# Gated linear attention and a feed-forward layer on one core: the first two pairs' loads as single transfers of one unit, v of pair 0 in f32

## The chip, the core and the metric

The kernel runs on one core of a Trainium2 chip. The core has five engines with queues of their own, each in order: TensorE (PE in the profile; PEld is its weight load), VectorE (DVE), ScalarE (ACT), GpSimd (POOL) and SyncE (SP). Transfers between memory and the core are issued from SP, ACT or POOL and carried out by 16 DMA engines that all queues share; a transfer that changes the type (f32 to bf16) is issued from POOL here. The metric is the device time of one execution in microseconds (us), median over runs.

## The reference

Inputs are q, k, v and alpha of shape (4 batches, 8 heads, 768 tokens, 48), f32, with alpha between 0.8 and 1, and the two weights of the feed-forward layer.

```python
for t in range(S):
    state = alpha[:, :, t, :, None] * state + np.einsum('bhd,bhe->bhde', k[:, :, t], v[:, :, t])
    y[:, :, t] = np.einsum('bhd,bhde->bhe', q[:, :, t], state)
...
x = y.transpose(0, 2, 1, 3).reshape(3072, 384)
h = x @ w_in                                    # 384 x 2048
g = 0.5 * h * (1 + tanh(sqrt(2 / pi) * (h + 0.044715 * h**3)))
out = g @ w_out                                 # 2048 x 384
```

## The kernel before

**Tiling.** The 768 tokens are cut into 6 chunks of 128. A *unit* is one chunk of one batch (all 8 heads), a *pair* is one chunk of two batches: 12 pairs, numbered 0 to 11, pairs 0 and 1 being chunk 0. Within a chunk the recurrence is done by matrix products. For each unit: the logarithm of alpha (`la`, L302 or L304, ACT), its cumulative sum over tokens by a product with a triangle of ones (`cum`, PE), exponentials of the sum and of its negative (`b`, `binv`, L344, ACT), and of the chunk's total (`bend`); q times b and k times binv (`qp`, `kp`, L355, DVE); both transposed on PE (`qkT_ps`, L365) and copied to SBUF (`qkT`, L383, DVE or ACT); the scores k^T q (`at`, L426, PE), masked to the triangle on DVE (`atm`, L433, two instructions for a unit); y from scores and v, plus q times the state from chunk 1 on (`yps`, PE); y cast to bf16 (`x`, L490), transposed (`xT_ps`, L497) and copied to `xT` (L501). The state is carried on by `kv` (L443) and `st` (L468). The feed-forward layer works on a block of one pair: eight groups of six products of layer 1 (`hT`, L508) with a gelu each (`gT`, L514, ACT), and layer 2 (`acc`, L527) with result and store.

**Order.** A small planner in the file (`Scheduler`, L40) is given every task with an engine, a cost and a priority; it puts them in order by its own cost table `W`, and the kernel issues each engine's instructions in that order. It also puts idle products (`fill`, L218) where it expects PE to wait. So a change of the tasks or of `W` changes the static order of every engine.

**Pairs 0 and 1** (`PACKED`). Their a, q and k are stored in a packed way: a partition holds four tokens of two heads, so that one row of a transfer is 768 B (four tokens of 48 f32) in place of 192 B. `load_packed` (L239) brings a pair's tensor in four pieces of 32 partitions (98 KB each, two pieces for each batch). The two halves in which the packed pair is worked through (`parts`, L202) are halves of the heads and not units: each holds data of both batches, so everything needs all four pieces (`rows_of`, L601). `ut_blk` and `blk` are the triangles and the sum for this packing: blocks of 32 x 32. The transposed q and k are put back in order of units and tokens when they are copied to `qkT` (L383), and k is transposed back for `kv` (`k_ps` L391, `kn` L398).

**Loads.** `RINGS` (L147) lists the pieces that SP and ACT issue at the start: a and q of pair 0 alternate between SP and ACT, k of pair 0, a and q of pair 1 are SP's. `TABLE` says that ACT loads its table of functions after its last issue. `LOADS` (L144) is POOL's list: a gate that waits for the last piece of a of pair 0, then v of pair 0 (cast to bf16); a gate on k of pair 0; the first quarter of w_in; k of pair 1 in four pieces; and so on through weights and later pairs, whose a, q, k come as rows of 192 B. A gate (`wait`, L253) is a tiny copy on POOL that reads the tile waited for.

**PSUM.** The cumulative sum of pair 0 takes one tile of tag `ca` for both halves; pair 1's takes two of tag `ff` (`CUM_FF`, L147).

Of the kernel before, what the change touches and what calls it, by code (L numbers as in the profile page):

```python
# [17 lines left out]
    qk2=910, qk1=500, ev8=650, ev4=350, mask=640, st=1090, st0=545, end=110, attn2=590, xc=520, xe=330, ot=540,  # L18
    ev8_act=960, ev4_act=520, xc_act=450, xe_act=450, ot_act=450,
    strip=2120, cast=1500, weight=2080, dma=2100, issue=1100, wissue=760, sp=100, store=2600, turn=1250, landed=2200, xbar_qk=1500, xbar_x=1000, late_x=2500, piece=330, late_k=1500, piece_issue=450, begin=2700, cast_0=1300, share=1200, cast_1=1900, ln_packed=1040, cold=380, fill=216, zero=1100,  # L20
# [116 lines left out]
class _Kernel:  # L137
# [6 lines left out]
    LOADS = ('gatea0', 'v0', 'gatek0', 'in 0', 'pk1', 'in 1', 'in 2', 'v1', 'in 3', 'out 0', 'out 1', '2a', 'out 2', '2b', 'out 3', '3', '4', '5', '6', '7', '8', '9', '10', '11')  # L144

    PACKED, CUM_FF, R = (0, 1), (1,), 4
    RINGS = (('a', 0, 0, 'SP'), ('a', 0, 2, 'ACT'), ('a', 0, 1, 'SP'), ('a', 0, 3, 'ACT'), ('q', 0, 0, 'SP'), ('q', 0, 2, 'ACT'), ('q', 0, 1, 'SP'), ('q', 0, 3, 'ACT'), ('k', 0, 0, 'SP'), ('k', 0, 2, 'SP'), ('k', 0, 1, 'SP'), ('k', 0, 3, 'SP'), ('a', 1, 0, 'SP'), ('a', 1, 1, 'SP'), ('a', 1, 2, 'SP'), ('a', 1, 3, 'SP'), ('q', 1, 0, 'SP'), ('q', 1, 1, 'SP'), ('q', 1, 2, 'SP'), ('q', 1, 3, 'SP'))  # L147
    TABLE = ('q', 0, 3)
# [9 lines left out]
                a=4, q=4, k=4, v=6)  # L158
# [68 lines left out]
    def load(self, n, c, i, lo=0, hi=2):  # L227

        nc, C, H, D = self.nc, self.C, self.H, self.D
        u = self.p[c, i]  # L230

        def emit(e):
            if n not in u:
                u[n] = self.tile(n, [C, 2, H, D], BF16 if n == "v" else F32)
            src = self.src[n][2 * i + lo:2 * i + hi].rearrange("b h s d -> s (b h) d")[c * C:(c + 1) * C]
            (nc.sync if e == "SP" else nc.gpsimd).dma_start(u[n][:, lo:hi].rearrange("t b h d -> t (b h) d"), src)  # L236
        return emit

    def load_packed(self, n, c, i, j):  # L239

        nc, C, H, D, R = self.nc, self.C, self.H, self.D, self.R
        u = self.p[c, i]

        def emit(e):
            if n not in u:
                u[n] = self.tile(n, [C, 2, H, D], F32)
            src = self.src[n][2 * i + j // 2, j % 2 * 4:j % 2 * 4 + 4, c * C:(c + 1) * C]
            {"SP": nc.sync, "ACT": nc.scalar}.get(e, nc.gpsimd).dma_start(  # L248
                u[n][32 * j:32 * j + 32].rearrange("g i (o r) d -> g (i o) (r d)", o=2),
                src.rearrange("y (g r) d -> g y (r d)", r=R))  # L250
        return emit
# [75 lines left out]

    def exp(self, u, n, lo, hi):
        D, H = self.D, self.H

        def emit(e):
            if n == "bend":
# [3 lines left out]
                if u["packed"]:  # L336
                    out = u[n].rearrange("f i (w z) -> f z (i w)", z=2)[:, lo]
# [37 lines left out]
    def turned(self, u, i, which):  # L375
        def emit(e):
            t = self.qkT(u)[:, :, i]
            t = t if which == "qk" else t[:, "qk".index(which)][:, None]
            ps = u.pop(("T_ps", i, which))
            if u["packed"]:  # L380
                t = self.qkT(u)[:, "qk".index(which)].rearrange("f i (w z) (g r) -> f z (i w) g r", z=2, r=self.R)[:, i]
                ps = ps[:, 0].rearrange("f r (w g) -> f w g r", g=32)
            self.copy(e)(t, ps)  # L383
# [53 lines left out]
    def kv(self, u, i):  # L437
        nc, H, C, D = self.nc, self.H, self.C, self.D

        def emit(e):  # L440
            kv = u["kv", i] = self.tile("yk", [C, H // 2, 2 * D], F32, "kv")
            for p in range(H // 2):
                nc.tensor.matmul(kv[:, p, :], u["kn" if u["packed"] else "kp"][:, i, 2 * p:2 * p + 2, :].rearrange("t h d -> t (h d)"),  # L443
                                 u["v"][:, i, 2 * p:2 * p + 2, :].rearrange("t h d -> t (h d)"),
# [27 lines left out]
    def y(self, u, i, c, b):  # L472
        nc, H, C, D = self.nc, self.H, self.C, self.D

        def emit(e):
# [6 lines left out]
            for h in range(H):  # L482
                nc.tensor.matmul(y[:, h, :], u["atm", i][:, h % 2, h // 2, :], u["v"][:, i, h, :],  # L483
# [64 lines left out]
    def tasks(self):  # L548
# [9 lines left out]
        def load(key, cost, emit):  # L558
            nonlocal n
            land = W[{"v": "cast", "w": "weight"}.get(key[0], "strip")]  # L560
            loads[key] = s.add("load", {"POOL": cost}, n, emit, gate, land=W[f"cast_{key[1]}"] if key[0] == "v" and key[1] in self.PACKED else land * 3 // 8 if key[0] != "w" and key[1] in self.SPLIT else land,
                               late=W["share"] if key[:2] == ("v", 0) else 0)
# [13 lines left out]

        for r, m, j, e in self.RINGS:
            loads[r, m, j] = s.add("load", {e: W["piece_issue"]}, n, self.load_packed(r, *pairs[m], j), land=W["piece"] + (0 if n else W["begin"]))
            n += 1
            if (r, m, j) == self.TABLE:  # L580
                s.add("table", {"ACT": W["table"]}, n, lambda e: self.act_set(LN_EXP))
        for step in self.LOADS:
            if step[0] == "v":
                rows(int(step[1:]), "v")
            elif step[0] == "p":
                r, m = step[1], int(step[2])
                for j in range(4):
                    loads[r, m, j] = s.add("load", {"POOL": W["piece_issue"]}, n, self.load_packed(r, *pairs[m], j), gate, land=W["piece"] + (0 if j else W["late_k"]))
                    n += 1
            elif step[:4] == "gate":  # L590
                key = step[4], int(step[5]), int(step[6:] or 3)
# [9 lines left out]
        def rows_of(r, m, j):  # L601
# [135 lines left out]
        n = 0  # L737
# [112 lines left out]
```

## Time and profile before

| | us |
|---|---|
| median of 5 runs | 181.93 (181.44 to 182.51) |
| the profiled execution | 182.64 |
| its span in the profile | 180.9 |

| engine | busy, us | share of the span |
|---|---|---|
| PE | 173.4 | 96% |
| PEld | 130.3 | 72% |
| ACT | 129.5 | 72% |
| DVE | 96.6 | 53% |
| POOL | 60.8 | 34% |

The chain of work that ended last is made of PE for 88%, of DMA for 6% and of SP's queue for 2%. PE's busy time includes 9.0 us of idle products (24 of them, nearly all in the first 26 us).

When the loads of POOL's queue land (issue and landing in us):

| transfer | issued | landed |
|---|---|---|
| v, pair 0 | 4.62 | 11.5 |
| w_in, first quarter | 7.93 | 14.5 |
| w_in, second quarter | 10.90 | 17.8 |
| v, pair 1 | 12.42 | 21.0 |
| w_in, fourth quarter | 14.86 | 23.4 |
| w_out, first and second quarter | 15.60, 16.4 | 25.2, 27.2 |
| a, second unit of pair 2 | 23.63 | 33.0 |
| w_out, fourth quarter | 29.76 | 37.0 |
| a, q, k of pair 3 | 30.52, 31.68, 32.82 | 38.7, 40.6, 42.4 |

A line of the timeline or of the chain begins with its start and its length in us; behind it stand engine, line, operation and, in brackets, the idle time before it with what ended it. A line of the table by windows has, for a stretch of time, the busy time of each engine with its number of instructions, then the clock granted to PE, the share of the DMA engines, and the GB/s that they moved.

### The profile page before, as it was taken

To read this page: it belongs to the slowest core of one execution; us is meant where nothing else is said; L and a number is where in the kernel's file an instruction comes from. 1 tells how busy PE (TensorE), PEld (TensorE's weight loads), DVE (VectorE), ACT (ScalarE), POOL (GpSimd) and SP (SyncE) were. 2 spreads that over 40 slices of the span, in tenths; PEclk is the share of its full clock that TensorE was granted. 3 is DMA by queue.
4 is the path that set the end of the run, shared out by engine and by line. 5 is a ranking of instruction groups with operands and counts; after the bars stand their busy time and mean duration, and the time that the engine had idled before them with its cause. 6 is when DMAs were issued, how large, how long until landed. Compare 5 with 4: busy or idle time off the path is not lost.

```text
span 180.9 us, 4489 instructions
## 1 busy us (share of the span) xinstructions
PE 173.4 (96%) x1858; PEld 130.3 (72%) x1861; DVE 96.6 (53%) x201; ACT 129.5 (72%) x214; POOL 60.8 (34%) x68
## 2 busy tenths in 40 slices
PE   7877999999999999999999999999999999999993
PEld 2555869765796788688688779678677687685872
DVE  7384863045669696487499798299254425000000
ACT  3556868965898678848888757888987984491841
POOL 2597738977566766330740500000000000000000
DMA  5999999999999999998994535443361270311102
GB/s 158 183 246 227 187 239 226 228 214 206 192 312 207 193 264 223 196 240 220 115 235 134 134 95 137 82 127 81 63 155 59 44 205 4 87 43 47 43 0 87
DMA packets 51204, 27.75 MB, mean 153 GB/s; under 512 B 38832, under 2 KB 48240, under 8 KB 51184
## 3 DMA queue, kind: packets, MB, share of 16 engines
q0 software_dynamic: 32096, 17.70, 63.4%
q1 hardware_dynamic: 18512, 9.38, 19.7%
q10 hardware_dynamic: 576, 0.39, 0.7%
q8 instruction: 14, 0.23, 0.6%
q14 instruction: 6, 0.05, 0.1%
HBM read 25.17 MB, written 4.72 MB: 165 GB/s over the span
## 4 chain that ended last, share of the span: by engine, by line
PE 88%; DMA 6%; SPq 2%; DVE 1%; ACT 1%; ACTq 0%; issue 0%; DVEq 0%
PE hT L508 35%; PE acc L527 34%; DMA q<-in_q_dram 6%; PE qkT_ps L365 4%; PE at L426 4%; PE yps L483 3%; PE kv L443 2%; PE cum L321 2%; PE yps L480 2%; SPq L248 2%; PE xT_ps L497 1%; PE cum L323 1%; DVE qp L355 1%; PE idle L223 1%; PE k_ps L391 1%; ACTq L248 0%
## 5 line engine op out<-in xcount | busy, mean ns | idle before, releaser
L508 PE MATMUL hT<-xT,w_in 128*128 128x256 bf16 x576 | 69.5, 273 | 0.0
L527 PE MATMUL acc<-w_out,gT 128*128 128x384 bf16 (+1 forms) x400 | 69.1, 319 | 0.0
L514 ACT ACTIVATE gT<-hT 128x512 bf16<-128x512 f32 x96 | 56.7, 598 | 16.4 <-PE hT L508 13.1
L508 PEld LDWEIGHTS <-w_in 128*128 128x128 bf16 x576 | 54.3, 98 | 6.9
L527 PEld LDWEIGHTS <-gT 128*128 128x128 bf16 x400 | 36.6, 97 | 19.3
L433 DVE TENSOR_TENSOR atm<-at,ut 128x512 bf16<-128x512 f32 x48 | 30.0, 683 | 13.6 <-PE at L426 13.6
L355 DVE TENSOR_TENSOR qp<-q,b 128x768 bf16<-128x768 f32 (+1 forms) x15 | 11.9, 796 | 26.5 <-ACT b L344 24.4
L236 POOL DMA_DIRECT2D v<-in_v_dram x13 | 14.6, 1123 | 12.8 <-PE xT_ps L497 9.0
L539 ACT COPY ot<-acc 128x384 f32<-128x384 f32 (+1 forms) x18 | 8.3, 460 | 13.8 <-PE acc L527 12.9
L236 POOL DMA_DIRECT2D q<-in_q_dram x11 | 12.3, 1114 | 12.5 <-DVE xT L501 7.1
L236 POOL DMA_DIRECT2D a<-in_alpha_dram x11 | 12.2, 1114 | 6.0 <-ACT la L304 1.9
L344 ACT ACTIVATE b<-cum 128x768 bf16<-128x768 f32 (+1 forms) x15 | 10.3, 684 | 5.2 <-PE cum L293 2.6
L214 ACT ACT_TABLE_LOAD x9 | 11.5, 1283 | 2.8 <-issue 2.6
L236 POOL DMA_DIRECT2D k<-in_k_dram x11 | 12.2, 1111 | 3.1 <-DMA w_out<-in_moe_w_out_dram 1.2
L355 DVE TENSOR_TENSOR kp<-k,binv 128x768 bf16<-128x768 f32 (+1 forms) x15 | 11.9, 791 | 0.1
L514 ACT ACT_TABLE_LOAD x9 | 11.5, 1283 | 0.2
L490 ACT CAST x<-yps 128x384 bf16<-128x384 f32 x15 | 7.2, 479 | 5.3 <-PE yps L483 5.2
L223 PE MATMUL idle<-zero 128*128 128x512 bf16 x24 | 9.0, 473 | 1.3 <-DVE half L798 1.2
L344 ACT ACTIVATE binv<-cum 128x768 bf16<-128x768 f32 (+1 forms) x15 | 10.2, 683 | 0.0
L383 DVE COPY qkT<-qkT_ps 128x1024 bf16<-128x1024 bf16 (+1 forms) x12 | 7.9, 687 | 3.6 <-PE qkT_ps L365 3.6
L465 DVE TENSOR_TENSOR stmp<-kv,st 128x384 f32<-128x384 f32 x16 | 8.8, 552 | 1.2 <-PE kv L443 1.2
L468 DVE TENSOR_TENSOR st<-stmp,ends 128x384 bf16<-128x384 f32 x16 | 8.9, 558 | 0.6
(64 smaller groups left out, 160.7 us busy)
## 6 DMA issues: line engine op xcount, KB each, us to landing
out_dram<-ot SPq DMA_DIRECT2D x23, 192.0 KB, 2.3
a<-in_alpha_dram POOLq DMA_DIRECT2D x9, 384.0 KB, 10.7
q<-in_q_dram POOLq DMA_DIRECT2D x9, 384.0 KB, 11.3
k<-in_k_dram POOLq DMA_DIRECT2D x9, 384.0 KB, 11.5
v<-in_v_dram POOLq DMA_DIRECT2D x11, 192.0 KB, 11.3
w_in<-in_moe_w_in_dram POOLq DMA_DIRECT2D x4, 384.0 KB, 7.4
w_out<-in_moe_w_out_dram POOLq DMA_DIRECT2D x4, 384.0 KB, 10.2
a<-in_alpha_dram SPq DMA_DIRECT2D x6, 96.0 KB, 3.5
```

What stands on the lines that cost most here:

```text
L214: nc.scalar.add_instruction(mybir.InstLoadActFuncSet(name=nc.get_next_instruction_name(), act_func_set_id=i, engine=mybir.EngineType.Activ ...
L223: self.nc.tensor.matmul(ps, self.zero[:, 0:self.C], self.zero, start=True, stop=True)
L236: (nc.sync if e == "SP" else nc.gpsimd).dma_start(u[n][:, lo:hi].rearrange("t b h d -> t (b h) d"), src)
L344: self.nc.scalar.activation(u[n].rearrange("t i h d -> t i (h d)")[:, lo:hi], cum, AF.Exp, scale=1.0 if n == "b" else -1.0)
L355: self.nc.vector.tensor_tensor(out, rows, b, op=ALU.mult)
L433: self.nc.vector.tensor_tensor(u["atm", i][:, o], u["at", i][o], self.ut[:, None, :].to_broadcast([self.C, self.H // 2, self.C]), op=ALU.mult)
L465: nc.vector.tensor_tensor(s, acc, old, op=ALU.add)
L468: nc.vector.tensor_tensor(new.rearrange("f p (o d) -> f (p o) d", o=2), acc.rearrange("f p (o d) -> f (p o) d", o=2), ends, op=ALU.mult)
L508: self.nc.tensor.matmul(h[:, s], self.w_in[:, j, (nt + s) * self.C:(nt + s + 1) * self.C], self.xT[c][:, j, lo:hi].rearrange("p g t -> p ( ...
L514: return lambda e: self.nc.scalar.activation(self.gT[c % self.NG][:, nt:nt + 2, lo * self.C:hi * self.C], f.pop(("h", c, lo, nt)), AF.Gelu ...
L527: self.nc.tensor.matmul(f["acc", c, b][:, lo:hi], self.gT[c % self.NG][:, nt, b * self.C:(b + 1) * self.C], self.w_out[:, nt, lo:hi], star ...
L539: self.copy(e)(f["ot", c, b][:, sl], f["acc", c, b] if half is None else f["acc", c, b, half][:, sl])
```

## The change

- a, q and k of pairs 0 and 1 come as one transfer for each unit, 128 partitions of 1536 B in rows of 768 B, all issued from SP. The packing is another: within a unit, partition 4g + j holds tokens 4g to 4g + 3 of heads 2j and 2j + 1. So the two parts of a packed pair are now its two units, and each part's ln, sums, products, transposes and copies need that unit's transfers only. `rows_of` and `load_packed` are gone, and the scores of a unit wait for that unit's copies and no longer for all four.
- SP's list: pair 0: a of unit 0, a of unit 1, q0, k0, q1, k1, then v of both units as one transfer in f32 (393 KB in rows of 192 B), then pair 1: a0, a1, q0, k0, q1, k1. ACT issues no transfer.
- v of pair 0 is cast on the core, one unit at a time (`narrow`, by ACT or DVE as the planner says). v of pair 0 is no longer in POOL's list; nor is k of pair 1. POOL has one gate, on v of pair 0, ahead of the first quarter of w_in.
- pair 0's cumulative sums take two tiles of tag `ff`.
- `ut_blk` and `blk` are made by one reduction and two operations on 128 x 128 from the triangle and the identity.

```diff
-    LOADS = ('gatea0', 'v0', 'gatek0', 'in 0', 'pk1', 'in 1', 'in 2', 'v1', 'in 3', 'out 0', 'out 1', '2a', ...
+    LOADS = ('gatev0', 'in 0', 'in 1', 'v1', 'in 2', 'in 3', 'out 0', 'out 1', '2a', ...
-    PACKED, CUM_FF, R = (0, 1), (1,), 4
-    RINGS = (('a', 0, 0, 'SP'), ('a', 0, 2, 'ACT'), ('a', 0, 1, 'SP'), ('a', 0, 3, 'ACT'), ('q', 0, 0, 'SP'), ...
+    PACKED, CUM_FF, R = (0, 1), (0, 1), 4
+    RINGS = (('a', 0, 0, 1), ('a', 0, 1, 2), ('q', 0, 0, 1), ('k', 0, 0, 1), ('q', 0, 1, 2), ('k', 0, 1, 2), ('v', 0, 0, 2),
+             ('a', 1, 0, 1), ('a', 1, 1, 2), ('q', 1, 0, 1), ('k', 1, 0, 1), ('q', 1, 1, 2), ('k', 1, 1, 2))
+    NARROW = (0,)
...
+            if u["packed"] and n != "v":
+                dma(u[n][:, lo].rearrange("p (o r) d -> p o (r d)", o=2),
+                    src[0, :, c * C:(c + 1) * C].rearrange("h (g r) d -> g h (r d)", r=R))
...
+    def narrow(self, u, lo, hi):
+        def emit(e):
+            if "vb" not in u:
+                u["vb"] = self.tile("vb", [self.C, 2, self.H, self.D], BF16)
+            self.copy(e)(u["vb"][:, lo:hi].rearrange("t b h d -> t (b h d)"), u["v"][:, lo:hi].rearrange("t b h d -> t (b h d)"))
+        return emit
...
-                t = self.qkT(u)[:, "qk".index(which)].rearrange("f i (w z) (g r) -> f z (i w) g r", z=2, r=self.R)[:, i]
-                ps = ps[:, 0].rearrange("f r (w g) -> f w g r", g=32)
+                t = t[:, 0].rearrange("f j (g r) -> f j g r", r=self.R)
+                ps = ps[:, 0].rearrange("f r (g j) -> f j g r", j=4)
...
+            if m == 1:
+                cums[1].deps.append(ys[1, 0])
...
+            if m in self.NARROW:
+                vin = [s.add("vb", {"DVE": W["vb"], "ACT": W["vb_act"]}, P + 19, self.narrow(u, j, j + 1), vin[j:j + 1]) for j in range(2)]
...
-        nc.vector.memset(self.blk, 0.0)
-        for t in self.ut_blk:
-            nc.vector.memset(t, 0.0)
-        for p in range(4):
-            nc.vector.memset(self.blk[32 * p:32 * p + 32, p:p + 1], 1.0)
-        for p in range(4):
-            a, b = 32 * p, 32 * p + 32
-            nc.vector.tensor_copy(self.ut_blk[1][a:b, a:b], self.ut_h[a:b, a:b])
-            nc.vector.tensor_copy(self.ut_blk[0][a:b, a + 1:b], self.ut_h[a:b, a:b - 1])
+        nc.vector.tensor_reduce(self.blk, self.ident.rearrange("p (g j) -> p j g", j=4), axis=mybir.AxisListType.X, op=ALU.max)
+        same = self.blk[:, None, :].to_broadcast([C, C // 4, 4])
+        nc.vector.tensor_tensor(self.ut_blk[1].rearrange("p (g j) -> p g j", j=4), self.ut_h.rearrange("p (g j) -> p g j", j=4), same, op=ALU.mult)
+        nc.vector.tensor_tensor(self.ut_blk[0], self.ut_blk[1], self.ident, op=ALU.subtract)
```

The planner's order of the start is thereby another:

| engine | order after the change, up to layer 1 and a little beyond |
|---|---|
| ACT | table, ln u0, ln u1, b and binv u0, b and binv u1, bend, copy of kT u0, **cast of v u0**, copy of a transposed tile of u1, **cast of v u1**, ln of pair 1 twice, x u0, b and binv of pair 1 by unit, copy of qT, table, gelu |
| DVE | qp and kp u0, copy of qT u0, qp and kp u1, ends, mask u0, copy of a transposed tile of u1, mask u0, masks u1, xT u0, x u1, qp of pair 1 u0, xT u1, kp of pair 1 u0, kn, qp and kp of pair 1 u1 |
| PE | 6 fills, sums u0, sums u1, 2 fills, transposes u0, 3 fills, scores u0, transposes u1, 4 fills, scores u1, y u0, sums of pair 1 u0, xT u0, y u1, sums of pair 1 u1, xT u1, 1 fill, transposes of q of pair 1 u0, of k of pair 0, then layer 1 |
| POOL | gate on v, w_in first and second quarter, v of pair 1, w_in third and fourth quarter, w_out first and second, pair 2 and so on as before |

From layer 1's third group of block 1 on, PE's order is the same as before.

## The prediction

> **What bounds the kernel now.** I read the page first, then the chain of waits in order of time, then the timeline of the first 36 us, then the DMA issues with their landing times.
>
> ```profile
> PE 173.4 (96%) x1858; PEld 130.3 (72%) x1861; DVE 96.6 (53%) x201; ACT 129.5 (72%) x214; POOL 60.8 (34%) x68
> PE   7877999999999999999999999999999999999993
> ```
>
> PE is full from the fifth slice on (a slice is 4.5 us). Only the first 29 us can give anything: whatever makes PE's dense part begin earlier is won, as long as the loads keep up.
>
> ```profile
> 1.67 3.91 DMA q<-in_q_dram
> ...
> 8.88 6.82 DMA q<-in_q_dram
> ...
> 15.83 1.03 DVE qp L355 x2
> ...
> 17.18 0.65 PE qkT_ps L365 x8
> 17.82 0.66 PE hT L508 x6
> ...
> 29.49 3.93 PE hT L508 x36
> ```
>
> This is the chain of waits (start, length, what). Pair 1's q, issued from SP at 8.88, lands at 15.7. DVE stands in it with qp, and the copies of xT are queued behind qp, so layer 1 (hT, L508) begins at 17.7. Between 17.2 and 29.5 PE is nearly gapless (some 0.9 us of fills at 24.2 to 25.5); at 29.49 begin the last six groups of block 1.
>
> ```profile
> 4.01 0.94 ACT L302 ACTIVATE la<-a 128x384 f16<-128x384 f32 x2
> 6.99 0.49 ACT L344 ACTIVATE b<-cum 128x384 bf16<-128x384 f32 x1 [2.04 <-PE cum L293]
> 7.48 0.18 POOL L256 COPY gate<-k 128x1 f32<-128x1 f32 x1 [1.58 <-DMA k<-in_k_dram]
> 11.82 0.94 ACT L302 ACTIVATE la<-a 128x384 f16<-128x384 f32 x2 [1.02 <-DMA a<-in_alpha_dram]
> 16.77 0.61 DVE L501 COPY xT<-xT_ps 128x384 bf16<-128x384 bf16 x2
> 35.37 0.94 ACT L304 ACTIVATE la<-a 128x384 f16<-128x384 f32 x2
> 41.52 0.85 ACT L304 ACTIVATE la<-a 128x768 f16<-128x768 f32 x1
> ```
>
> The timeline: ln starts when all four pieces of a are there (4.01), and the first exponential waits for the cumulative sums of both units (6.99).
>
> **Prices.** Transfers in rows of 768 B, almost alone on the wires:
>
> ```profile
> 2.00:3.00 1.00, 1.00 (x4) 0.43 (x3) 0.96 (x8) 0.36 (x1) 0.00 (x0) 1.00 0.92 281
> 3.00:4.00 1.00, 1.00 (x4) 0.33 (x3) 0.91 (x8) 0.92 (x1) 0.00 (x0) 1.00 0.96 262
> 13.00:14.00 1.00, 1.00 (x22) 0.86 (x20) 0.71 (x2) 0.68 (x2) 0.60 (x1) 1.00 1.11 341
> ```
>
> The last column is GB/s. A unit is 128 x 1536 B = 197 KB: 0.72 us at 273, between 0.58 (at 341, the best stretch) and 0.76 (SP's and ACT's queue in the first 20 us: 1.57 MB in 30.2% of them). A landing shows about 0.75 us after its last byte: a's 393 KB are moved by 3.3 and ln starts at 4.01. The first bytes come at about 2.0.
>
> v of pair 0 in f32 is 393 KB in rows of 192 B on SP's queue, which the trace does not have. Nearest is POOL's queue with rows of that size and kind: a, q, k of pair 3 land at 38.7, 40.6 and 42.4, 1.85 us each. From below: 341 GB/s gives 1.15. From above: v as it is now, 6.9 us from issue (4.62) to landing (11.5), of which another queue had a share. I take 1.85, the same rows. The Trainium skill (DMA: Bandwidth & Descriptors, Specifications) speaks against this part: it asks for transfers of at least 512 B and says that smaller ones are read, changed and written back. If that doubled the row's 1.85 us, v would come 1.85 us later and the gain below would shrink to about 1.2. No row here shows it on SP's queue; the 1.85 us of POOL's 192 B rows already hold whatever it costs there.
>
> A quarter of a weight: 2.0 us (w_out's first two land at 25.2 and 27.2).
>
> **The change part by part.** *Loads.* Thirteen issues on SP at 0.43 us replace twenty on SP and ACT and, on POOL, four and the cast of v: 5.6 us of SP, which does nothing else. Six are out by 3.4 us while their bytes need until 6.3; SP's waits are for landings eight transfers back, which come in time. Nothing is queued behind but stores from 45 us on. ACT loses four issues (1.85 us), so its table load ends near 2.1, not 3.9, ahead of any data. Units seen by 0.72 us steps: a0 3.4, a1 4.15, q0 4.9, k0 5.6, q1 6.3, k1 7.05, v at 8.1 + 0.75 = 8.8. Pair 1 follows alone until w_in starts at about 10, then shares: a 9.6 and 10.4, q 11.4, k 12.7, q 14.0, k 15.4.
>
> *Unit 0's chain.* ln 3.45 to 3.95. Its cumulative sum starts at 4.0, not 5.0: six fills at 0.43 (the rate of the first nine) end by 3.8. Packed sums take 0.89 at full rate; the fills run at half rate until about 5, so I pay 1.4 for this one: until 5.4. The Trainium skill (TensorE: Matmul & The Clock Gate, Part 1) has the half rate end after about 3.4 us of work, at a moment that varies; by it the sum could end some 0.25 earlier (an estimate: half rate until 1.19 + 3.4), and the later steps, which wait for v and w_in, would not move. b of unit 0 starts at 5.5 instead of 6.99 because pair 0's sums now lie in tiles of their own. DVE multiplies q at 6.05 and k at 6.5 (0.55 each), four transposes each (0.39), copies of 0.69 on DVE and 0.59 on ACT end at 7.8 and 8.15; scores of unit 0 at 8.2, not 10.75.
>
> *v.* ACT's order now has two casts of v, and the first stands ahead of unit 1's copy of kT: v at 8.8, cast to 9.35 (0.48, as x L490), copy to 9.9, scores of unit 1 at 10.1, masks (0.64 each) to 11.9. The second cast ends at 10.3, and behind it are pair 1's ln: 10.3 to 11.2 instead of 11.82 to 12.76. Cost: 0.96 us of ACT, in cover of DVE's masks while v is there by 8.8; each us that v is late delays kT, ln and everything after by as much, and POOL's gate too.
>
> *To layer 1.* y of unit 0 10.7, its cast 11.15 to 11.65, y of unit 1 11.95, pair 1's second sum 12.25 to 13.15, xT of unit 1 transposed 13.1. On DVE the cast of x (0.56) and qp of pair 1 (its q landed at 11.4) end at 13.5, the last xT copy at 13.8. So hT could begin at about 14.1.
>
> *w_in.* POOL's gate moves from k0 (7.48) to v, 8.85; the first quarter is issued at 9.25 instead of 7.93. Alone on the wires from 10 it would be seen at 12.8; with all of pair 1 ahead, at 8.1 + 4.3 + 2.0 + 0.75 = 15.2. It shares, and no cast of v is ahead of it in POOL's queue any more (that one landed at 11.5, w_in at 14.5): 14.8, so hT starts at 14.85, 2.8 before its present 17.66. All bytes to the fourth quarter: 2.0 + 4.3 + 1.85 + 4.3 + 8.0 + 1.6 (v of pair 1) + 0.75 = 22.8, now 23.4; its group, the seventh, comes at about 22.9.
>
> *To the dense part.* The new order has three fills in place of four between there and block 1; two groups of layer 1 go ahead of pair 1's k. Following the order with the same durations, block 1's third group starts at 26.45 instead of 29.49: 3.0 us. I take 0.3 off because I passed each hand-over at 0.05 us, and some rows show 0.1 to 0.15 (DVE after PE at 25.26 to 25.30, ACT to DVE 15.71 to 15.83). From there PE's order is the same as before.
>
> *Set-up.* Fifteen small DVE copies and memsets (0.06 to 0.17 each) become a reduction and two 128 x 128 operations: before DVE's first real work at 6.05, hidden; even 1 us more would be. Evacuations read another stride with the same number of elements: nothing taken.
>
> *Loads after it.* Pair 2's second a lands at 33.0 and is used at 35.84, pair 3's at 38.7 and 41.52: slack 2.9 and 2.8, w_out's last quarter 37.0 and 44.25. With 2.7 us won these still fit, since the bytes in front shrink by 0.6 us. They cap the gain near 3.4. In the later part of POOL's list a load of v stands one to three places from where it was; the loads around it (pair 4's a lands at 45.8 and is used at 57.1) have 10 us of room, so nothing is taken for it.
>
> **Sum.** 182.64 (span 180.9 and 1.74 around it) - 2.7 = 179.9 for an execution like the profiled one; the median is 0.71 below that one: 181.93 - 2.7 = **179.2**. Fast ends of the prices (0.58 per unit, v 1.15) would give 4 us by the chain, capped at 3.4 to 3.6 by pair 2's loads: 178.3.
>
> **Rivals.** (1) *The transfers set the pace anyway.* Total bytes hardly shrink, and w_in starts 1.3 us later. If POOL's queue gets the small share, w_in is seen at 16 or later, the fourth quarter at 23.4 as now, and pair 2's ln waits: gain 0.6 to 1.5, time 180.4 to 181.3. For it: w_in now takes 6.6 us from issue to landing. Against: a cast of v was ahead of it then. (2) *v is late, moderately*: seen near 11.5, w_in near 17.6: nothing won, 181.5 to 182.4. (3) *Slower: v in f32 as a plug.* It is one transfer in front of pair 1 in SP's queue, in front of kT and ln in ACT's order, and in front of POOL's gate. By the order above, hT starts at v + 6.0 to 6.4 us, and block 1 as late as before when v is seen at 12.0, that is when its 2048 rows take 5.0 us on SP's queue. At 6.9, the far row above, it is seen at 13.9: +1.8 us, 183.7. For it: nothing shows such small rows on that queue. Against: POOL's same rows go in 1.85 with all 16 engines. That the units do not stand alone is excluded by the order of waits: each ln, product and sum waits for its own transfer.
>
> **Chances.** Forecast (178.3 to 180.4) 0.59, rival 1 0.15, rival 2 0.09, rival 3 0.17. A median of this kernel can be told from another by about 0.3%, 0.55 us. Faster: forecast and rival 1, 0.74; within 0.09; slower 0.17. The range 178.3 to 181.8 leaves out rival 3 and the last of rival 2.
>
> **What would show it.** In the new trace: first b near 5.5, v's cast at 8.8 to 9.3, scores of unit 1 near 10.1, pair 1's ln near 10.3, hT near 14.9 waiting for w_in by a few tenths at most, block 1's last six groups near 26.5 to 26.8, no gap on PE at pair 2's sums (36 now, 33.3 then). Wrong if ACT idles ahead of the cast of v until 10 or later, or hT waits for w_in beyond 16.

## The result, and the profile after

The changed kernel takes 183.42 us (median of 28 executions, 181.28 to 185.35), the kernel before 181.75 (47 executions, 181.11 to 183.03). The ratio is 1.0053 [1.0035, 1.007]: slower by 0.5%, where 1.5% faster was forecast. Here and below a ratio leaves out the executions that are over 1.5% above the fastest of their kernel (8 of the 28, all with a low clock); the medians over all executions lie 0.9% apart. The profiled execution took 181.6 us, one of the fastest of its kernel, with a span of 179.8; the one shown of before, 182.64, was one of the slower of its kernel. So these two must not be subtracted; they are read for where the waits are.

The page of the changed kernel, busy time of the engines and PE in 40 slices:

```profile
PE 171.4 (95%) x1851; PEld 129.5 (72%) x1854; DVE 97.3 (54%) x191; ACT 129.9 (72%) x214; POOL 57.2 (32%) x62
...
PE   6986799999999999999999999999999999999993
```

PE is full from the sixth slice on. The second and third slices (of 4.5 us) have risen from 8 and 7 to 9 and 8; the fourth and fifth, 13.5 to 22.5 us, have fallen from 7 and 9 to 6 and 7. Chain of waits of the changed kernel, in order of time (start, length, what):

```profile
4.82 4.71 DMA v<-in_v_dram
...
9.59 0.18 POOL gate L249
9.77 0.81 POOL w_in L256
10.58 8.54 DMA w_in<-in_moe_w_in_dram
...
19.16 0.83 PE hT L507 x6
...
28.51 3.93 PE hT L507 x36
```

q of pair 1 and DVE, which made up the chain before, are gone from it. It now runs from v on SP's queue through POOL's gate into w_in. The last line is the dense part. From its start to the end of the span it is 151.3 us here and 151.4 before (180.9 - 29.49), and 151.3 to 151.6 in the profiled executions below whose chain shows that line. The time is decided by when this line starts; nothing after it was won or lost.

The timeline of the changed kernel up to layer 1 (idle time before the instruction and its cause in brackets):

```profile
5.30 0.49 ACT L343 ACTIVATE b<-cum 128x384 bf16<-128x384 f32 x1 [0.49 <-PE cum L286]
8.01 0.40 PE L425 MATMUL at<-qkT 64*128 64x128 bf16 x8
9.55 0.51 ACT L325 CAST vb<-v 128x384 bf16<-128x384 f32 x1 [1.60 <-DMA v<-in_v_dram]
10.60 0.40 PE L425 MATMUL at<-qkT 64*128 64x128 bf16 x8 [0.69 <-ACT qkT L382]
13.86 0.36 DVE L500 COPY xT<-xT_ps 128x384 bf16<-128x384 bf16 x1
16.02 1.48 PE L507 MATMUL hT<-xT,w_in 128*128 128x256 bf16 x12 [1.37 <-DMA w_in<-in_moe_w_in_dram]
16.05 0.56 DVE L354 TENSOR_TENSOR qp<-q,b 128x384 bf16<-128x384 f32 x1 [0.93 <-DMA q<-in_q_dram]
17.98 0.56 DVE L354 TENSOR_TENSOR kp<-k,binv 128x384 bf16<-128x384 f32 x1 [1.38 <-DMA k<-in_k_dram]
19.16 0.83 PE L507 MATMUL hT<-xT,w_in 128*128 128x256 bf16 x6 [0.99 <-DMA w_in<-in_moe_w_in_dram]
```

The units do stand alone: the first exponential starts at 5.30 (6.99 before), the last copy of xT at 13.86 instead of some 17.1 (the second of the two that began at 16.77). Then PE stands for w_in's first quarter until 16.02, DVE for pair 1's q and k until 16.05 and 17.98, and the third group for w_in's second quarter until 19.16. So 3.2 us were won up to xT, and most of that is given back to three landings.

SP's own queue in the same timeline shows the cause of one of them:

```profile
5.47 3.06 SPq L240 DMA_DIRECT2D a<-in_alpha_dram  x2
...
10.55 0.62 SPq L240 DMA_DIRECT2D k<-in_k_dram  x1
```

An issue takes 0.61 us, not 0.43, and the first issue behind v's 2048 rows takes 2.40 of the 3.06. It waits for no landing: the waits of SP's queue in the trace show none in this stretch. Pair 1's last k is issued at 10.55 and lands at 17.85.

**The clock.** Each execution comes with the mean clock granted to PE. 11 of the changed kernel's 28 executions are at 0.999 or 1.000, with a median of 182.32 (181.28 to 183.45); 17 are at 0.981 to 0.991, 182.92 to 185.35. Of the kernel before, on the chip of the first experiments, 2 of 31 are below 0.998. A mean of 0.99 over 180 us is 1.8 us of clock lost, a mean of 0.981 twice that. The profiled execution is one at full clock and can't show what happens in the others.

### The profile page after: what moved, and what is told of

The parts are those of the page before. It is cut to its first block, busy times and chain, and to the rows that moved or that the text cites. A ratio compares the mean times of both kernels' runs of the same rounds, so it can differ in the third digit from the quotient of the medians.

```text
span 179.8 us, 4442 instructions
## 1 busy us (share of the span) xinstructions
PE 171.4 (95%) x1851; PEld 129.5 (72%) x1854; DVE 97.3 (54%) x191; ACT 129.9 (72%) x214; POOL 57.2 (32%) x62
## 4 chain that ended last, share of the span: by engine, by line
PE 87%; DMA 7%; SPq 2%; ACT 1%; POOL 1%; issue 0%
PE hT L507 35%; PE acc L526 35%; DMA w_in<-in_moe_w_in_dram 5%; PE at L425 4%; PE qkT_ps L364 3%; DMA v<-in_v_dram 3%; PE yps L482 3%; PE kv L442 2%; SPq L240 2%; PE cum L314 2%; PE yps L479 2%; PE xT_ps L496 1%; PE cum L316 1%; POOL w_in L256 0%; PE k_ps L390 0%
## 5 line engine op out<-in xcount | busy, mean ns | idle before, releaser
L432 DVE TENSOR_TENSOR atm<-at,ut 128x512 bf16<-128x512 f32 x48 | 30.4, 683 | 13.8 <-PE at L425 13.8
L243 POOL DMA_DIRECT2D q<-in_q_dram x11 | 12.3, 1114 | 13.7 <-DVE xT L500 7.1
L243 POOL DMA_DIRECT2D vb<-in_v_dram x12 | 13.3, 1111 | 9.1 <-PE xT_ps L496 5.2
L343 ACT ACTIVATE b<-cum 128x768 bf16<-128x768 f32 (+1 forms) x15 | 10.3, 684 | 3.5 <-PE cum L316 2.5
L215 ACT ACT_TABLE_LOAD x9 | 11.5, 1283 | 0.9 <-PEq L819 0.7
L513 ACT ACT_TABLE_LOAD x9 | 11.5, 1283 | 0.2
L382 DVE COPY qkT<-qkT_ps 128x1024 bf16<-128x1024 bf16 (+1 forms) x13 | 8.5, 685 | 2.7 <-PE qkT_ps L364 2.7
L489 ACT CAST x<-yps 128x384 bf16<-128x384 f32 x13 | 6.2, 476 | 4.4 <-PE yps L482 4.4
L489 DVE CAST x<-yps 128x384 bf16<-128x384 f32 x11 | 6.1, 557 | 5.7 <-PE yps L482 5.6
## 6 DMA issues: line engine op xcount, KB each, us to landing
a<-in_alpha_dram POOLq DMA_DIRECT2D x9, 384.0 KB, 11.5
```

The costliest lines, as they stand in the source:

```text
L215: nc.scalar.add_instruction(mybir.InstLoadActFuncSet(name=nc.get_next_instruction_name(), act_func_set_id=i, engine=mybir.EngineType.Activ ...
L243: dma(u[t][:, lo:hi].rearrange("t b h d -> t (b h) d"), src.rearrange("b h s d -> s (b h) d")[c * C:(c + 1) * C])
L343: self.nc.scalar.activation(u[n].rearrange("t i h d -> t i (h d)")[:, lo:hi], cum, AF.Exp, scale=1.0 if n == "b" else -1.0)
L432: self.nc.vector.tensor_tensor(u["atm", i][:, o], u["at", i][o], self.ut[:, None, :].to_broadcast([self.C, self.H // 2, self.C]), op=ALU.mult)
L489: self.copy(e)(x, u["y", i].rearrange("t h d -> t (h d)"))
L513: return lambda e: self.nc.scalar.activation(self.gT[c % self.NG][:, nt:nt + 2, lo * self.C:hi * self.C], f.pop(("h", c, lo, nt)), AF.Gelu ...
```

## The experiments

The letters in the expectations: theory A is that v, as one f32 transfer on SP's queue, is a plug (pair 1 behind it in the queue, w_in behind the gate), and that PE, standing for w_in, loses its clock. B puts the low clock readings on the start of the execution. D: pair 1 and w_in share the wires, so what one gains the other loses. Ratios are to the kernel before, run on the same chip.

**The change once more, unedited.**

> The changed kernel as it is. In the 28 executions so far the mean granted clock of PE was 1.000 or 0.999 (181.3 to 183.5 us), 0.989 to 0.991 (183.0 to 184.5) or 0.981 (184.4 to 185.4). Theory A (the weights are late; while PE stands for them, its clock is taken down in some executions for a stretch worth some 1.7 us): the same three groups again, median 183 to 183.8, and a trace in which hT waits some 2.4 us for w_in. Theory B (PE's clock drops because the start has fewer idle products, 6 + 2 + 3 + 4 before the first y and gaps between them): the same here. Theory C (the spread has nothing to do with the clock, the loads alone vary): the times vary as much within the executions at 1.000 as over all.

184.29 us (8 executions), ratio 1.0061 [1.0008, 1.0115], 6 of 8 below full clock, and this time the profiled one is of that kind (184.37, span 182.6, clock 0.99). PE's timeline, then its windows (us, PE busy and instructions, granted clock, DMA share, GB/s):

```profile
18.30 2.41 PE L507 MATMUL hT<-xT,w_in 128*128 128x256 bf16 x12 [3.84 <-DMA w_in<-in_moe_w_in_dram]
```
```profile
18.00:19.00 1.00, 0.69 (x5) 0.85 2.22 170
...
20.00:21.00 1.00, 1.00 (x9) 0.50 1.38 197
...
22.00:23.00 1.00, 1.00 (x14) 0.95 1.25 203
```

w_in's first quarter, issued at 9.52, lands at 18.3, 2.3 later than in the first profile. PE stands 3.84 us; then the clock is halved for some 3.4 us (0.85 in one window, 0.50 in the three from 19 to 22, 0.95 in the next: 0.15 + 3 x 0.50 + 0.05 is 1.7 us lost), and the twelve products take 2.41 instead of 1.48. The dense part starts at 31.29, 2.8 later: less than 2.3 and 1.7 together, since the third group no longer waits for the second quarter (0.99 in the first profile). One late landing is thus paid twice: by the standing and by the clock after it.

**Filling the standing.** Idle products into the tile of layer 1's first and third group.

```diff
+            for _ in range({0: 6, 4: 4}.get(nt, 0) if (c, lo) == (0, 0) else 0):
+                self.nc.tensor.matmul(h.rearrange("p s t -> p (s t)"), self.zero[:, 0:self.C], self.zero, start=True, stop=True)
```

> Adds 6 idle products ahead of layer 1's first group and 4 ahead of its third, in the time that PE stands there for w_in (1.37 and 0.99 us in the trace); nothing else is changed. Theory A: PE no longer stands long there, the mean clock is 0.999 or more in nearly all executions, and the median falls by 1.0 to 1.7 us, to 181.7 to 182.4. Theories B and C: the clocks and the median stay as in the changed kernel, within 0.4 us.

183.18 (12), ratio 1.0042 [1.0014, 1.007]. Only 2 of 12 are below full clock, where the unedited kernel had 23 of 36 in its two series. The standing takes the clock down. But the executions at full clock have a median of 182.9, no less than those of the unedited kernel: in the profile the quarter lands at 17.6 and hT still stands 1.71. The fills cure the second payment, not the first.

**Filling the start.** Three more idle products among the first fills.

```diff
-            for _ in range(n):
+            self.fills = getattr(self, "fills", 0) + 1
+            for _ in range(n + {1: 1, 4: 2}.get(self.fills, 0)):
```

> Adds one idle product to the first fill (7 in place of 6, over the 0.4 us that PE stands before the first sum) and two to the fourth (6 in place of 4, over the 0.7 us before the scores of unit 1); the waits for w_in stay. Theory B: the mean clock is 0.999 or more in nearly all executions and the median falls by 1.0 to 1.7 us. Theory A: the clocks and the median stay as in the changed kernel, within 0.4 us. Theory C: the same as A here.

183.02 (12), ratio 1.0038 [1.001, 1.0066], 6 of 12 below full clock: B is not supported. (Its profiled execution had a mean clock of 0.759 and is not read.)

**w_in not behind v.** POOL's gate on k of unit 1.

```diff
-    LOADS = ('gatev0', 'in 0', 'in 1', ...
+    LOADS = ('gatek0', 'in 0', 'in 1', ...
...
-        return lambda e: self.nc.gpsimd.tensor_copy(self.gate[:, 0:1], u[r][:, 0, 0, 0:1])
+        return lambda e: self.nc.gpsimd.tensor_copy(self.gate[:, 0:1], u[r][:, j, 0, 0:1])
```

The second part, by which the gate reads the unit that is meant, stands in every edit below with a gate on `a` or `k`.

> POOL's gate ahead of w_in waits for k of unit 1 of pair 0 (landed at 7.95) in place of v (9.53); the order of the other engines is the same. Theory A: the first quarter of w_in is issued 1.4 us earlier and lands near 14.6 in place of 16.0, the second near 18; hT begins near 14.9, PE stands less than 1 us for w_in, block 1's last six groups begin 0.6 to 1.2 us earlier (27.3 to 27.9), the clock is low less often, median 181.3 to 182.5. Rival D (the wires are full, what w_in gains v and pair 1's units lose): v lands after 10.5, the scores of unit 1 and pair 1's ln come later, hT begins no earlier than 15.7 and the median stays at 183 or above.

183.35 (12), ratio 1.007 [1.0039, 1.0102]. DVE's timeline:

```profile
14.45 0.56 DVE L354 TENSOR_TENSOR qp<-q,b 128x384 bf16<-128x384 f32 x1 [1.27 <-DMA q<-in_q_dram]
...
19.71 0.56 DVE L354 TENSOR_TENSOR kp<-k,binv 128x384 bf16<-128x384 f32 x1 [0.60 <-DMA k<-in_k_dram]
```

The quarter is issued at 8.16 and lands at 14.7, nearly the predicted 14.8, but pair 1's last k lands at 19.6, 9.3 us after its issue, and the dense part starts at 29.60. What w_in gains, pair 1 loses: D, though v, which D had late too, still lands by 9.3.

**v back on POOL's queue.** v as in the kernel before (cast by the transfer, behind a gate on a of unit 1), w_in's gate on k of unit 1; the rest of the change stays.

```diff
-    LOADS = ('gatev0', 'in 0', ...
+    LOADS = ('gatea0', 'v0', 'gatek0', 'in 0', ...
-    RINGS = (..., ('v', 0, 0, 2), ...
+    RINGS = (..., 
-    NARROW = (0,)
+    NARROW = ()
```

> Undoes the part with v: v of pair 0 is cast by its transfer from POOL again, after a gate on a of unit 1, and w_in waits for k of unit 1 of pair 0 as in the kernel before; units and packing stay as changed, and the planner orders the engines anew. Theory E (v's 2048 rows hold up SP for 2.4 us, so that pair 1's units are on the wires together with w_in, which is issued late): SP issues pair 1's units by 9 without a stop, k of pair 1 lands by 15.5, the first quarter of w_in by 15, block 1's last six groups begin near 28, the clock is full in nearly all executions, median 180.6 to 181.6. Rival D (the bytes ahead of layer 1 set the pace whatever queue they take): w_in at 16 or later, dense part from 28.8 or later, median 181.8 to 183.

181.29 (12), ratio 0.999 [0.9969, 1.0012], 11 of 12 at full clock. With v undone, w_in no longer behind it and the engines' orders planned anew, 0.6% is won, and the clock. hT starts at 16.32 with no wait for w_in (landed 15.4). What ends late is another thing, in ACT's timeline:

```profile
10.80 0.52 ACT L295 ACTIVATE la<-a 128x384 f16<-128x384 f32 x1 [1.55 <-DMA a<-in_alpha_dram]
```
The planner has put pair 1's ln ahead of unit 1's last copy on ACT; ACT stands for pair 1's a, and the scores of unit 1 come at 12.61 instead of 10.60.

**v in f32 from ACT's queue.** All orders kept; v is issued from ACT after unit 1's ln.

```diff
+            if t is self.v0:
+                continue
             t.emit(t.engine)
+            if t is self.ln1:
+                self.v0.emit("ACT")
```

> v of pair 0 in f32 is issued by ACT, behind ln of unit 1 (about 4.8, as on SP), in place of SP; everything else and every engine's order stay. Theory E: SP's stop of 2.2 to 2.9 us behind v is gone, pair 1's units are issued by 9, the dip of the transfers between 8 and 9 us goes, k of pair 1 lands at 16 or before (17.9 and more now); v lands at 9.5 to 10.5, w_in no later than now; median falls by 0.7 to 1.5 us. Rival D: v lands later by what pair 1 gains, w_in at 16 to 18 as now, median within 0.5 us of the changed kernel.

182.36 (12), ratio 1.0043 [1.0022, 1.0064], 7 of 12 below full clock. SP's stop is gone (pair 1 issued by 8.7), yet v, now beside pair 1 instead of ahead of it, lands at 11.63. ACT's timeline:

```profile
11.65 0.51 ACT L325 CAST vb<-v 128x384 bf16<-128x384 f32 x1 [3.44 <-DMA v<-in_v_dram]
```
This is rival 3 of the prediction at nearly its break-even of 12.0: v late delays the copy behind its cast, the scores of unit 1 (12.70), and the gate (w_in issued at 11.80, landed 17.0). The second quarter lands at 20.1 and ends last.

**The first quarter of w_in early.** Its issue behind a gate on a of unit 1, before v's gate.

```diff
-    LOADS = ('gatev0', 'in 0', 'in 1', ...
+    LOADS = ('gatea0', 'in 0', 'gatev0', 'in 1', ...
```

> The first quarter of w_in alone goes ahead, after a gate on a of unit 1 (landed near 4.2); the gate on v then holds the rest of POOL's list. Orders of the other engines are the same. Theory A (PE's standing for the first quarter is what costs, and takes the clock down): it lands by 11, PE no longer stands 1.4 to 3.8 us there, the clock is full in nearly all executions, and pair 1's k or the second quarter ends last; dense part from 28 to 29, median 181.2 to 182.3. Rival D: q, k of unit 1, v and pair 1 all come later by the 2 us of w_in's bytes, scores of unit 1 at 12 or later, median 183 or more.

183.27 (12), ratio 1.0043 [1.0012, 1.0075], 11 of 12 below full clock. The quarter lands at 10.8, long before its use. v lands at 11.99 and the two issues behind it take SP 4.76 us (3.06 in the changed kernel; the first alone 3.70 and 2.40), so PE stands 2.16 us for the scores of unit 1 and the next sums run at half clock (1.44 instead of 0.82). D again, with v as the loser.

**The second quarter held back.** A second gate, on pair 1's last k, ahead of it.

```diff
-    LOADS = ('gatev0', 'in 0', 'in 1', ...
+    LOADS = ('gatev0', 'in 0', 'gatek1', 'in 1', ...
```

> A second gate, on pair 1's last k, holds POOL's second quarter of w_in and all behind it; the rest is the same. If the second quarter takes wire time from pair 1's units (rival D's reading of their 6 to 9 us from issue to landing), pair 1's k lands at 16.5 or before and the first quarter at 16 or before, while the second lands at 20 or later and PE stands for it instead: median within 0.7 us of the changed kernel. If the units are late because SP issued them late (theory E), k lands at 17.5 or later all the same, and the second quarter's lateness comes on top: median 0.5 to 2 us above the changed kernel.

187.19 (6), ratio 1.0267 [1.0222, 1.0312]. Much worse, and the first quarter still lands at 18.4, pair 1's k at 18.7. One of its windows (us, then the busy time of PE, PEld, DVE, ACT, POOL, clock, DMA share, GB/s):

```profile
16.00:18.00 2.00, 0.00 (x0) 0.00 (x0) 0.30 (x1) 0.09 (x1) 0.00 (x0) 0.97 0.13 28
```

For two microseconds the wires are at 13% while both transfers are still out. From 17 to 18 us, 17 packets move, 8 of w_in and 9 of pair 1, and fill 7.4% of the 16 engines: little more than the share of one. So here the second quarter was not the competitor, and a landing is not total bytes over total rate: it comes with the last share of the slowest DMA engine. What held that engine up isn't settled.

**No v at all.**

```diff
+            if t == "v":
+                nc.gpsimd.memset(u[t], 0.0)
+                return
...
-        return lambda e: self.nc.gpsimd.tensor_copy(self.gate[:, 0:1], u[r][:, 0, 0, 0:1])
+        return lambda e: self.nc.gpsimd.tensor_copy(self.gate[:, 0:1], u["k"][:, 1, 0, 0:1])
```

> Leaves out the load of v of pair 0 (v is set to zero by POOL, so the tokens of pair 0 come out without their attention part) and takes POOL's gate from unit 1's k, which had landed at 7.95; every engine's order is that of the changed kernel. Theory A (v on SP's queue is the plug: 2048 rows that stop SP by 2.4 us, and the gate behind it): SP issues pair 1's last k by 8.2 instead of 10.55, pair 1's q and k of unit 1 land by 14.5, w_in's first quarter is issued at about 8.2 and lands by 15, hT starts by 15.2, the last six groups by 27.2, and executions at full clock take about 180.2, 1.3 less than those of the changed kernel; at most a quarter of the executions are below full clock. Rival D (pair 1's bytes and w_in share the wires whatever v does; w_in's quarter or pair 1 ends last): w_in or the last k still lands at 16 or later, the last six groups start at 28.2 or later, executions at full clock take 181 or more, and half of the executions are below full clock.

181.85 (12), ratio 1.0001 [0.9971, 1.0031]; executions at full clock 181.02, 6 of 12 below. SP issues pair 1's last k at 8.10 and w_in, now behind a gate on k of unit 1, goes out at 8.27, as A said, but PE's timeline has

```profile
16.26 1.49 PE L510 MATMUL hT<-xT,w_in 128*128 128x256 bf16 x12 [1.41 <-DMA w_in<-in_moe_w_in_dram]
```

a landing at 16.2, 7.9 us after its issue (16.0 with v), as D said. v and the gate behind it cost 0.5% (1.0053 to 1.0001; of the medians, 0.9% to 0.1%); without them there is still nothing won over the kernel before.

**v in larger rows.** The same 393 KB at the same place in 512 rows of 768 B.

```diff
+            elif t == "v":
+                dma(u[t].rearrange("t b h d -> t (b h d)").rearrange("t (x y) -> t x y", x=4),
+                    src[:, :, c * C:(c + 1) * C].rearrange("b h (g r) d -> g (b h) (r d)", r=R))
```

> v of pair 0 by the same single transfer at the same place of SP's queue, the same 393 KB, but in 512 rows of 768 B instead of 2048 of 192 B (each partition then gets other tokens' values, so the attention part of pair 0 is of permuted v); all orders are those of the changed kernel. Theory A1 (the number of rows stops SP): the issue of pair 1's first a behind v takes under 1.2 us instead of 2.40, v lands by 8.9, w_in's first quarter is issued by 9.2 and pair 1's last k lands by 16.2; hT by 16, last six groups by 28, executions at full clock 0.5 to 1.2 less than the changed kernel's. Theory A2 (393 KB in front of pair 1 in whatever rows): the stop stays above 2 us, v lands at 9.3 or later, pair 1's last k at 17.3 or later, last six groups at 28.4 or later, time within 0.4 of the changed kernel's.

182.86 (12), ratio 1.004 [1.0012, 1.0068], 8 of 12 below full clock. SP's queue, and the chain of waits:

```profile
5.47 1.29 SPq L240 DMA_DIRECT2D a<-in_alpha_dram  x2
```
```profile
4.82 4.87 DMA v<-in_v_dram
...
16.90 2.17 PE hT L510 x12
```

The stop is gone (1.29 for the two issues behind v, not 3.06): it is the cut into 2048 small rows that stops SP, as A1 said (number and size of the rows go together here), and pair 1's q and k are no longer waited for. But v lands no earlier (9.69, with 192 B rows 9.53), and w_in, issued at 9.86, no earlier either (16.9): as A2 said of the time. What the small rows cost was the queue behind them. The Trainium skill (DMA: Bandwidth & Descriptors, Specifications) has transfers under 512 B read, changed and written back; these two landings do not show it.

**Pair 1's q and k left out.** v, gate and orders as changed.

```diff
+            if n in ("q", "k") and u["m"] == 1:
+                return
...
```

Both are set to zero at the start, so y of pair 1 comes out as zero.

> Leaves out the loads of q and k of pair 1 (both set to zero by POOL at the start, so the attention part of pair 1 comes out as zero); v, the gate, w_in and every engine's order stay as in the changed kernel. Theory S (w_in's first quarter is late because pair 1's q and k share its wires): v lands near 9.5, the quarter is issued at 9.7 and lands by 14.4, that is 4.7 after its issue instead of 6.3 to 8.7; hT starts at 14.5, the last six groups by 27.2, executions at full clock take about 180.3 (181.3 to 183.4 in the changed kernel) and at most a quarter of them are below full clock. Theory Q (the quarter needs its 6 us or more from issue on POOL's queue whatever else is on the wires): it lands at 15.7 or later, hT stands 1.3 or more, last six groups at 28.2 or later, 181.3 or more, and half of the executions are below full clock.

180.88 (12), ratio 0.9941 [0.9918, 0.9964], all 12 at full clock. PE's timeline:

```profile
15.12 1.49 PE L513 MATMUL hT<-xT,w_in 128*128 128x256 bf16 x12 [0.20 <-DMA w_in<-in_moe_w_in_dram]
```

The quarter, issued at 9.98, lands at 15.1: 5.1 after its issue, against 6.3 to 8.7. That is S rather than Q, short of S by some 0.4 us: sharing the wires with 787 KB of pair 1 makes it late. (Where v came from ACT's queue, and pair 1's last k was landing 1.3 us after the quarter's issue, it took 5.2.) With them gone, neither the standing nor the loss of clock appears; the second quarter is still waited for (1.10 us, the third group at 18.38).

**A version that beats both.** v on POOL's queue as above, and pair 1's ln behind the copies of pair 0's unit 1 (`prev`) in the planner's order; first with v's gate on a of unit 1, then on a of unit 0 (the last two lines, against the first version).

```diff
+            if m == 1:
+                for x in lns[1]:
+                    x.deps += prev
...
-    LOADS = ('gatea0', 'v0', 'gatek0', ...
+    LOADS = ('gatea00', 'v0', 'gatek0', ...
```

> v of pair 0 back with POOL's casting transfer as in the run that undid it (gate on a of unit 1 ahead of it, on k of unit 1 ahead of w_in), and pair 1's ln behind the copies of pair 0's qT and kT in the planner's order. If what that run still lost was ACT standing for pair 1's a ahead of unit 1's last copy: scores of unit 1 at about 10.6 instead of 12.61, y of unit 0 when v lands at 12.0, hT at 15.0 to 15.5, when w_in's first quarter lands, last six groups by 27.3, and 180.4 (0.9 less than that run, 1.2 less than the kernel before). If v's landing at 12 or the quarter at 15.4 ends last all the same: hT at 16 or later, last six groups at 28, 181.1 to 181.5.

> The same, with the gate ahead of v on a of unit 0 instead of unit 1, so that v is issued at about 4.0 instead of 4.8. If v is what unit 0's y waits for: v lands at 11.2, y of unit 0 then, and up to 0.5 less than the run with the gate on unit 1's a, 179.9 to 180.4. If v, sharing the wires earlier, delays the units in SP's queue (rival D): k of unit 1 lands at 8.4 or later instead of 7.95, scores of unit 1 0.4 later, and the time is the same or up to 0.5 more, 180.4 to 181.

> The best kernel once more (v by POOL's casting transfer behind a of unit 0, pair 1's ln behind pair 0's copies), for its interval and its clock. If it is faster than both others by its order: 179.9 to 180.4, a ratio of 0.990 to 0.994 to the kernel before, and at least ten of twelve executions at full clock. If the six executions of its first run were lucky: 181 or more, a ratio above 0.996, and several executions below full clock.

Gate on unit 1's a: 180.65 (12), ratio 0.9929 [0.9908, 0.9949], 10 of 12 at full clock. The scores of unit 1 lost their wait, but v, issued at 4.86, landed at 13.7 in the profile and y of unit 0 stood 2.19 us for it. Gate on unit 0's a: 180.05 (6), ratio 0.9922 [0.9895, 0.9949], and repeated 180.16 (6), ratio 0.9906 [0.9871, 0.994]; all 12 executions at full clock, 179.69 to 181.22. The first one's chain:

```profile
4.16 4.08 DMA k<-in_k_dram
...
15.03 0.82 PE hT L507 x6
...
26.59 3.93 PE hT L507 x36
```

v is issued at 3.85 and lands at 10.9, the quarter at 8.83 and 14.9, so hT starts at 15.03 with no transfer in front of it, and the dense part at 26.59. k of unit 1 (8.24, 0.3 later than in the changed kernel, with v beside it) now stands at the head of the chain. In the repeated run's profile the quarter landed at 16.2 and hT stood 1.48: the spread of that landing is still there. The clock was not lost by it in any of the 12, while the run without v stood as long (1.41) in its profile and lost it in 6 of 12. Why is not settled, since the executions without a profile can't be looked into; in the two profiles PE was busy for 0.55 and 0.59 of the step of the clock with the wait in it, which costs nothing by the table further down. PE's order differs too: here pair 1's products stand between single groups of layer 1, there twelve products come at once.

| kernel | w_in, 1st quarter: issued, landed | last six groups start | ratio to before |
|---|---|---|---|
| before | 7.93, 14.5 | 29.49 | 1 |
| changed | 9.71, 16.0 | 28.51 | 1.0053 |
| changed again | 9.52, 18.3 | 31.29 | 1.0061 |
| gate on k of unit 1 | 8.16, 14.7 | 29.60 | 1.0070 |
| no v | 8.27, 16.2 | 27.58 | 1.0001 |
| v in 768 B rows | 9.86, 16.9 | 29.88 | 1.0040 |
| no q, k of pair 1 | 9.98, 15.1 | 27.73 | 0.9941 |
| v by POOL, gate on a of unit 0 | 8.83, 14.9 | 26.59 | 0.9922 |

The second and third columns are of one profiled execution each; the last has the ratios given above, over the executions of the run.

## Why the prediction was wrong

**Right.** *The units' chain*: b at 5.30 (predicted 5.5), scores of unit 0 at 8.01 (8.2), of unit 1 at 10.60 (10.1), pair 1's ln at 10.86 (10.3), y of unit 0 at 10.94 (10.7), the last xT copy 13.86 to 14.2 (13.8). *v's landing*: 9.53 (8.8), its issue to landing 4.7; late by 0.7, far from the break-even at 12.0. *The set-up and the loads after it*: no wait for pair 2's a; 151.3 us from the dense part on, as before.

**Wrong, the step that decides: the first quarter of w_in, "14.8, so hT starts at 14.85".** The term was sized as 2.0 us of wire beside a share of pair 1, with first bytes 0.75 us after the issue at 9.25. Measured: 16.0, 18.3, 17.6, 16.9 in four profiled executions of three kernels with the same gate, 6.3 to 8.7 after the issue. Three causes are shown. The start: in the changed kernel's trace the first packet of POOL's queue moves at 11.5, 1.8 us after the issue (from 9.7 to 11.5 only SP's queue moves any), and in the runs with this gate it comes 1.6 to 2.1 after it; without pair 1's q and k, too, it takes 1.6. That is 1.1 us more than the term has; hT is late by 1.2 in the first profile. Sharing: without pair 1's q and k the quarter lands 5.1 after its issue. And, in one execution, the uneven end: with the wires at 13% it still took until 18.4. This is rival 1 ("seen at 16 or later") at a dearer price than its 180.4 to 181.3.

**Wrong: the 5.6 us of SP.** The count of issues was right, and the waits did come in time. The price was 0.61 instead of 0.43, and nothing in the sum stood for the issue behind 2048 rows: 2.40 us, 3.70 where w_in ran beside it. So pair 1's q and k came at 16.0 and 17.85, not 14.0 and 15.4. Rival 3 had v in front of pair 1 in this queue, but put the price on v's landing instead of on the queue. The run with 768 B rows shows that this part alone is worth little: with the stop gone the ratio is still 1.004, because w_in ends last.

**Missing: the clock.** The text costed half rate only for the first products. It had no term for PE standing later, and in 17 of 28 executions that costs one or two stretches of about 1.7 us. At full clock the change is slower by 182.32 - 181.75 = 0.6 us, with all executions by 1.7. The rest is not all clock, since an execution that lost the clock has also stood longer: the fills, which keep the clock in 10 of 12 executions, bring the median from 184.29 to 183.18, back by 1.1 of the 2.3 us lost on that chip. The Trainium skill (TensorE: Matmul & The Clock Gate, Part 1) names the mechanism: the clock is halved after an idle window of about 3.4 us, counted in windows that run freely. The 3.84 us row agrees. Waits of 2.09 and 2.16 us also lost the clock here and one of 2.19 did not, so the length alone does not decide.

What does is in the traces. In each that shows a change of the granted clock, it changes only at steps of 3.41 us, counted from its first rise, and where the steps lie differs from execution to execution. Counted in these steps (PE's busy share of one, then the clock in the next):

| run | step, us | PE busy | clock after it |
|---|---|---|---|
| changed again, wait 3.84 | 15.28 to 18.69 | 0.11 | 0.50 |
| first quarter early, wait 2.16 | 9.90 to 13.31 | 0.35 | 0.50 |
| v in 768 B rows, wait 2.09 | 14.12 to 17.54 | 0.39 | 0.50 |
| standing filled, wait 1.71 | 14.97 to 18.38 | 0.50 | 1.00 |
| v from ACT's queue, wait 2.14 | 8.32 to 11.73 | 0.55 | 1.00 |
| v by POOL, gate on a of unit 1, wait 2.19 | 12.31 to 15.72 | 0.57 | 1.00 |

The two losses of the run with the second quarter held back follow steps of 0.01 and 0.34. So a step need not be idle to cost the clock: 0.39 was too little, 0.50 enough, and a wait of 2 us is paid twice or not by how it falls on the steps. The table is read off after the fact; no run was made to test it.

**Wrong: the base (an estimate).** The walk gave a start of the dense part at 26.45 plus 0.3, and its gain was counted from 29.49, in an execution 0.9 above its kernel's median (182.64 to 181.75). By the constant 151.4 and 1.8 around the span, the median of before starts its dense part near 28.6. The gain of the walk was thus 1.8, not 2.7, and the forecast should have stayed at its own 179.9. The best version bears this out: with a dense part from 26.59 its profiled execution takes 179.74, and its median is 180.05.

**Two readings of lines.** The fast bound of 0.58 us for a unit is from the window of 13 to 14 us, in which POOL's queue moved 0.26 MB and SP's rows of 768 B only 0.08. And the 1.57 MB in 30.2% of the first 20 us are SP's queue alone; ACT's is another 0.39 MB in 6.6%. Neither moves the sum.

## What to carry to other kernels

A transfer that leaves the critical path on paper has still to be followed to what it now stands in front of: list for each queue what is issued behind it, and count its rows as well as its bytes. Where several loads end at one wait of PE, their landings differed by 2 us between executions here; put work of PE under that wait, since a stand of 2 us or more can be paid a second time by the clock. A walk through one profiled execution gives an absolute time: compare it with the kernel's other executions before taking a difference from it.

## What was not expected of the hardware

- An issue of 256 rows took 0.61 us on SP; two issues behind a transfer of 2048 rows took 3.06, behind the same bytes in 512 rows 1.29.
- A transfer on POOL's queue can be out for 8 to 9 us with the wires at 13% for the last two (the quarter of w_in, issued 9.53, landed 18.4).
- The first bytes of a transfer on POOL's queue came 1.6 us or more after its issue (1.8 in the changed kernel: issued 9.71, first packet 11.5).
- After PE had stood 3.84 us the granted clock was 0.50 for three microseconds at a stretch, and twelve products took 2.41 us instead of 1.48. The clock also went after a step of 3.41 us in which PE was busy for 39%.
